# Later slots for the inverse-transform tables and a shifted forward burst in an FFT-mixing plus GELU-MLP kernel

## The chip, the cores and the metric

The kernel runs on one core of a Trainium2 chip. The metric is the device time of one execution in microseconds (us). The kernel before the change took 746.29 us, the median of three runs that lay between 744.68 and 748.18. A profiled execution took 745.42 us, 743.6 us of it from the first to the last instruction; its TensorE clock was granted in full over nearly the whole span.

In what follows PE is TensorE, ACT is ScalarE, DVE is VectorE, POOL is GpSimd and SP is SyncE, which here only issues DMAs.

## The reference, cut to what matters

```python
X = np.fft.rfft(x, axis=1)                       # x: (8, 3008, 256)
y = np.fft.irfft(X * (filt_r + 1j*filt_i), n=3008, axis=1)
h = y.reshape(24064, 256) @ w_in                 # w_in: (256, 2048)
out = (0.5*h*(1 + erf(h/sqrt(2)))) @ w_out       # w_out: (2048, 256)
```

Each of the eight batches is transformed along its 3008 positions, multiplied by a filter for each frequency and channel, and transformed back. The result goes, token by token, through a two-layer MLP with an exact GELU.

## The kernel before, in words

**The MLP.** The 24,064 tokens are cut into 47 tiles of 512. One tile is 16 steps of `mm1`: two matmuls of 512 columns into one PSUM bank (tag `h`, three banks), then a GELU on ACT that writes an f16 tile `g_sb` (L634, L637). The second layer of tile t runs while the first layer of tile t+1 does. For tile 0 it is the plain product, 64 matmuls of 256 columns (`mm2_first`, L647). From tile 1 on it is a seven-product scheme: 112 matmuls of 128 columns (`mm2_seven`, L706), fed by sums that DVE makes of `g_sb` (`sums_1` L675, `sums_2` L681, `sums_3` L688), with DVE combining the products into output tiles (L721 to L735). These use two PSUM banks with tag `o`, each in turn.

**The transforms.** 3008 = 47 x 64, so the transform of a batch is a chain of small matrix stages. Batch 0 is done ahead of the first tile. Each later batch is spread over the MLP tiles as bursts:

- `fold` (DVE, L106 and L107) makes sums and differences of the loaded input; `s1` (PE, L428) is the first stage. Its four PSUM banks, one of tag `h` and the three of tag `f`, are emptied two by DVE and two by ACT into `a_sb`, which SP writes to a DRAM scratch.
- `r1` reads it back in another order (`b_sb`, L444). `s2` (PE, L457) is the forward second stage. `s2_out` (DVE, L469) multiplies a bank of it by the filter `F` and writes a tile `p`. There are three such bursts for a batch, u = 0, 1, 2.
- `s3` (PE, L483) is the first inverse stage with the table `U`. `s3_out` empties its banks into `v_sb`, which goes to a second DRAM scratch (L496).
- `r2` reads that back (`d_sb`, L503). `s4` (PE, L512) is the last stage, with the table `T4a`; it writes 376 tokens of `y_sb`, from which `mm1` reads.

**The order.** It is written by hand. Time is cut into slots, 16 for a tile, and `put(slot, function, ...)` hangs a function on a slot. In each slot the functions hung there are issued first, then that slot's share of the second layer, then its `mm1`. One slot of the steady state issues 7 matmuls of the second layer and one `mm1`. Each engine works through its instructions in the order of issue, so an instruction that waits holds up all behind it on that engine. The bursts take the PSUM banks of tags `h` and `f` in turn, and wait until the earlier user's bank has been emptied.

**Tables made late.** `U` and the factors of `T4a` are needed only from batch 1 on. `table_4_factors` (L391: three small matmuls into one bank, three ACT copies) and `table_u` (L369: one matmul with `pick`, which POOL makes, and one ACT copy) run in tile 0, in slots 8 and 9, each in a bank of tag `o`. `mm2_first` begins at slot 9, also in the two `o` banks. `table_4_all` (POOL, L410 and L412) multiplies the factors out in four parts, from slot 10.

**Batch 1 and 2.** Tile 5 holds the last 448 tokens of batch 0 and the first 64 of batch 1. In slots 80 to 85 it has no `mm1`; the second layer of tile 4 takes 14 matmuls in each of these. Batch 1's third burst (`s2`, u = 2) is in slot 58, its `s3` in slot 67, and the `s4` of its first tokens in slots 80 to 83. Batch 2's folds are in slots 67, 69, 86 and 90, its `s1` in slots 89, 92, 96 and 100, and its first `s2` in slot 112.

Of the kernel before, what the change touches and what calls it, by code (L numbers as in the profile page):

```python
# [31 lines left out]
class _Mix:  # L32
# [332 lines left out]
        self.nc.gpsimd.tensor_scalar(out=self.pick, in0=to, scalar1=self.p, scalar2=None, op0=ALU.is_equal)  # L365

    def table_u(self):
        ps = self.bank("ps_u", "o")
        self.nc.tensor.matmul(ps[:, 0:128], lhsT=self.pick, rhs=self.u0.rearrange("p t r w -> p (t r w)"),  # L369
                              start=True, stop=True)  # L370
        self._evac(self.U.rearrange("p t r w -> p (t r w)"), ps[:, 0:128], "act")
# [15 lines left out]
                v.tensor_copy(out=self.T2g[:, r, :, j], in_=t[:, :, j, ::-1] if j else t[:, :, j])  # L387

    def table_4_factors(self, g):
        ps = self.bank("ps_t4", "o")  # L390
        mm = lambda o, n, t, k: self.nc.tensor.matmul(ps[0:96, o:o + n], lhsT=t, rhs=self.eye[0:k, 0:k], start=True, stop=True)  # L391
        for x in range(2):
            mm(NA * x, NA, self.T1g[:, x].rearrange("p r a j k -> p (r a j k)"), NA)
        mm(128, 128, self.T2g.rearrange("p r a j k -> p (r a j k)"), 128)
        t = self.t4
        self.G = t[:, 0:94].rearrange("p (x m) -> p x m", x=2)
        self.fcs = t[:, 96:224].rearrange("p (h w r) -> p w h r", h=2, r=2)
        self._evac(self.G[:, 0], ps[0:96, 0:NA], "act", self.wt[0:96])
        self._evac(self.G[:, 1], ps[0:96, NA:2 * NA], "act", self.wts[0:96])
        self._evac(t[:, 96:224], ps[0:96, 128:256], "act")  # L400
# [88 lines left out]
    def s3_out(self, b, u, i):  # L489
        ps = self.st[b, "ps3"][i]  # L490
        vt = self.pv.tile([128, 4, 256], BF16, tag="v", name="v_sb")
        for par in range(2):
            self._evac(vt[:, 2 * par:2 * par + 2, :].rearrange("p a b -> p (a b)"), ps[par],
                       "act")
        for q in range(2):
            self.nc.sync.dma_start(out=self.st[b, "R2"][:, 4 * u + 2 * i + q], in_=vt[64 * q:64 * q + 64])  # L496

# [277 lines left out]
def kernel(  # L775
# [9 lines left out]
    m = _Mix(ctx, tc, x, filt_r, filt_i, moe_w_in, moe_w_out, out)  # L785
# [4 lines left out]
    g = m.small  # L790
    wide = ctx.enter_context(ExitStack())
    m.psum(wide, w=(2, 1), m=(1, 1), n=(5, 1))
    act = "act"
# [109 lines left out]
    def put(slot, f, *a):  # L903
        at.setdefault(slot, []).append((f, a))

    def first(b):
        return (b * S // TCH) * 16

    busy, crowd, after = set(), set(), {}
    for b in range(1, B):  # L910
        hi = first(b)
        e = 4 * (b == B - 1)
        s1, n1, r1 = (4, 2.75, 16) if b == 1 else (hi - 87, 3.7, hi - 73) if b == 2 else (hi - 94 - e, 3.7, hi - 80 - e)
        s2 = (33, 45, 58) if b == 1 else (hi - 64 - 2 * e, hi - 48 - 3 * e + e // 4, hi - 32 - 3 * e)
        busy.update(range(s1 - 1, s1 + int(3 * n1) + 2))
        for c in range(4):
            slot = s1 + int(c * n1 + (b == 1 and c in (1, 2)))
            put((0, 1, 5, 8)[c] if b == 1 else (67, 69, 86, 90)[c] if b == 2 else s1 - 28 + e + 6 * c, m.fold, b, c)
            put(slot, m.s1, b, c)
            put(r1 if c < 3 else s2[0] + 1, m.r1, b, c)  # L920
        for u in range(3):
            put(s2[u], m.s2, b, u)
            for i in range(4):
                put(s2[u] + ((0, 2, 5, 6)[i] if b == u == 1 else 2 * i), m.s2_out, b, u, i // 2, i % 2)
            s3 = s2[u] + (9 if b == 1 and u != 1 else 10)
            put(s3, m.s3, b, u)
            put(s3 + 1, m.s3_out, b, u, 1)
            busy.update(range(s2[u] - 1, s2[u] + 5), range(s3 - 1, s3 + 2))
        after[b] = s3 + (5 if b > 1 else 4)
        crowd.update(range(s2[0], after[b]), range(s1 + 66, s1 + 94))  # L930
        if b + 1 < B:
            for i, (u, o, p) in enumerate(((0, 5, 2), (0, 7, 2), (1, 1, 4), (1, 5, 6), (1, 7, 6), (2, 1, 8), (2, 5, 10), (2, 7, 10))):
                put(s2[u] + o, m.load_next, b, p, i // 2, i % 2)

    for b in range(1, B):
        end = 1000000
        if b == B - 1:
            s4 = first(b) - 17
            for u in range(16):
                put(s4 + u, m.s4, b, u // 2, u % 2, act if u % 2 else False)  # L940
            for c in range(4):
                put(after[b] if c < 3 else s4 + 5, m.r2, b, c)
            continue
        for u in range(7, -1, -1):
            due = (b * S + GRP * u) // TCH * 16
            end = min(end, due - 2 if u or b > 1 else 81)
            if b == u == 1:
                end = 83
            for half in (1, 0):
                while end in busy:  # L950
                    end -= 1
                assert end > after[b] + 7
                put(end, m.s4, b, u, half, act if half or end in crowd or b == 1 and u == 0 else False)
                busy.add(end)
                end -= 1 if u < 3 else 2
            if u % 2 == 0:
                put(after[b] if u == 0 else end - 11, m.r2, b, u // 2)
# [2 lines left out]
    put(0, m.weights_4, g)  # L960
    put(0, m.table_u_pick, g)
    put(0, m.table_2_parities)
    put(8, m.table_4_factors, g)
    put(9, m.table_u)
    parts = [(w, h) for w in range(0, HB, 8) for h in range(2)]
    for i, slot in enumerate((10, 80, 96, 112)):
        put(slot, m.table_4_all, parts[2 * i:2 * i + 2])
    put(1, m.load_filters_again, nc.gpsimd, 0, 8)
    put(18, m.load_filters_again, nc.sync, 8, 16)
# [10 lines left out]
    for s in range((NT + 1) * 16):  # L980
        t, jc = s // 16, s % 16
        for f, a in at.pop(s, ()):
            f(*a)
        pace = lambda i: max(16 * (i - 6) // 10, 0) if t == late else i
        if t - 1 in seven:
            n = lambda i: (14 * i if i < 6 else 84 + 28 * (i - 6) // 10) if t == late else 7 * i
            m.mm2_seven(t - 1, n(jc), n(jc + 1))
        elif t < 2:
            n = lambda i: max(4 * i - 36, 0) if i < 16 else min(28 + 12 * (i - 16) // 5, 64)
            m.mm2_first(n(s), n(s + 1))  # L990
        for i in range(pace(jc), pace(jc + 1)) if t < NT else ():
            m.mm1(t, i)
# [31 lines left out]
```

## Time and profile before

| engine | busy us | share of the span |
|---|---|---|
| PE matmul | 722.8 | 97% |
| PE weight load | 507.2 | 68% |
| DVE | 583.1 | 78% |
| ACT | 575.5 | 77% |
| POOL | 292.9 | 39% |

The page gives for each engine the time in which it had an instruction at work, and the share of the span. Matmuls are pipelined, so a busy PE may still be waiting between starts. The timeline of one engine lists its instructions in order of time; a bracket at the end of a row gives the idle time ahead of it and what ended it. A table by stretches gives the busy time of every engine in each stretch of the span. Tile 0 begins at 38.5 us; the slots touched by the change lie between there and about 155 us.

A row of the timeline reads: start in us, duration in us, engine, line, operation, output and inputs, shape, how many; then, in brackets, the idle time before it and its releaser.

### The profile page before, as it was taken

The page shows a single profiled execution, that of the slowest core. Times are in us where ns is not written, and L with a number is a line of the kernel's source. Part 1 is how long each engine was busy: PE and PEld are TensorE (multiplying, and loading weights), DVE is VectorE, ACT ScalarE, POOL GpSimd, SP SyncE. Part 2 cuts the span into 40 slices and gives each one's busy share as a digit, 9 for nine tenths or more (in the row PEclk, how much of TensorE's full clock was granted, in tenths as well). Part 3 has the DMA queues.
Part 4 walks back from the last instruction along what each step waited for, and adds up shares of the span by engine and source line. Part 5 has one row for each costly group of instructions (what it writes and reads, how often), then busy time and mean ns, then how long its engine had stood idle before and what let it go on. Part 6 is the DMA issues. An engine that isn't in the chain of part 4 may idle for free.

```text
span 743.6 us, 20854 instructions
## 1 busy us (share of the span) xinstructions
PE 722.8 (97%) x8449; PEld 507.2 (68%) x8588; DVE 583.1 (78%) x1034; ACT 575.5 (77%) x1050; POOL 292.9 (39%) x546
## 2 busy tenths in 40 slices
PE   7989999999999999999999999999999999999997
PEld 4846666666776666666777666666677766777776
DVE  7876898888878797778976889778888887675666
ACT  6987777778887887778787777877788787777773
POOL 7994346675213453134611364115531112121121
PEclk9999999999999999999999999999999999999999
DMA  9999753746255652655536456255545443411011
GB/s 144 223 202 221 168 110 100 200 99 136 71 149 155 130 110 87 166 127 131 121 95 172 111 117 146 72 157 138 109 102 136 136 108 100 100 43 45 30 58 58
DMA packets 84051, 90.79 MB, mean 122 GB/s; under 512 B 13347, under 2 KB 63011, under 8 KB 83827
## 3 DMA queue, kind: packets, MB, share of 16 engines
q1 hardware_dynamic: 61011, 49.11, 25.7%
q0 software_dynamic: 22528, 40.15, 24.2%
q8 instruction: 67, 1.10, 0.6%
q14 instruction: 29, 0.24, 0.1%
q10 hardware_dynamic: 416, 0.20, 0.1%
HBM read 57.15 MB, written 48.23 MB: 142 GB/s over the span
## 4 chain that ended last, share of the span: by engine, by line
PE 82%; DMA 6%; ACT 5%; POOL 2%; DVE 2%; issue 2%; SPq 0%; DVEq 0%; POOLq 0%
PE ps_o L706 36%; PE ps_h L634 35%; PE ps_s L483 3%; PE ps_s L512 3%; ACT g_sb L637 3%; DMA x_sb<-in_x_dram 2%; PE ps_s L428 2%; PE ps_s L457 2%; ACT v_sb L329 1%; DMA d_sb<-R 1%; PE ps_o L647 1%; DMA F<-in_filt_i_dram 1%; POOL F L144 1%; ACT y_sb L329 1%; DMA R<-v_sb 1%
## 5 line engine op out<-in xcount | busy, mean ns | idle before, releaser
L637 ACT ACTIVATE g_sb<-ps_h 128x512 f16<-128x512 f32 x752 | 446.8, 602 | 148.4 <-PE ps_h L634 129.9
L634 PE MATMUL ps_h<-y_sb,w_in_sb 128*128 128x512 bf16 (+3 forms) x1465 | 417.1, 365 | 1.5 <-DVE a_sb L331 0.8
L753 POOL DMA_DIRECT2D out_dram<-ost x227 | 128.8, 574 | 387.1 <-DVE ost L735 366.2
L706 PEld LDWEIGHTS <-g_sb 128*128 128x128 f16 x2944 | 193.9, 98 | 82.0 <-issue 11.4
L706 PEld LDWEIGHTS <-s_sb 128*128 128x128 f16 x2208 | 148.0, 98 | 62.2 <-issue 11.1
L634 PEld LDWEIGHTS <-w_in_sb 128*128 128x128 bf16 x1600 | 125.1, 98 | 7.7 <-issue 2.1
L706 PE MATMUL ps_o<-w_sums,g_sb 128*128 128x128 f16 x1472 | 127.0, 219 | 0.9
L706 PE MATMUL ps_o<-w_sums,s_sb 128*128 128x128 f16 x1472 | 125.8, 219 | 1.6
L675 DVE TENSOR_TENSOR s_sb<-g_sb 128x1024 f16<-128x1024 f16 x184 | 120.9, 691 | 1.2 <-ACT g_sb L637 1.2
L706 PE MATMUL ps_o<-w_out_sb,g_sb 128*128 128x128 f16 x1472 | 119.2, 219 | 2.0 <-DVE ost L735 0.3
L469 DVE TENSOR_TENSOR p<-ps_s,F 128x1024 bf16<-128x1024 f32 x84 | 102.0, 1217 | 7.0 <-PE ps_s L457 5.4
L98 POOL DMA_DIRECT2D x_sb<-in_x_dram x156 | 79.0, 513 | 1.3 <-DMA x_sb<-in_x_dram 0.8
L728 DVE TENSOR_TENSOR t_sb<-t_sb,ps_o 128x256 f32<-128x256 f32 x46 | 19.3, 420 | 60.0 <-PE ps_o L706 60.0
L681 DVE TENSOR_TENSOR g_sb<-s_sb,g_sb 128x1024 f16<-128x1024 f16 x92 | 64.2, 699 | 1.6
L706 PE MATMUL ps_o<-w_out_sb,s_sb 128*128 128x128 f16 x736 | 63.8, 219 | 0.3
L688 DVE TENSOR_TENSOR s_sb<-g_sb 128x1024 f16<-128x1024 f16 x92 | 64.0, 696 | 0.0
L735 DVE TENSOR_TENSOR ost<-t_sb,ps_o 128x256 f32<-128x256 f32 x90 | 33.7, 415 | 21.1 <-PE ps_o L706 21.1
L512 PEld LDWEIGHTS <-d_sb 96*128 96x128 bf16 x448 | 31.8, 98 | 26.6 <-DMA d_sb<-R 0.9
L329 ACT ACTIVATE y_sb<-ps_s 128x376 bf16<-128x376 f32 x95 | 47.2, 497 | 1.6 <-PE ps_s L512 1.6
L329 ACT ACTIVATE v_sb<-ps_s 128x512 bf16<-128x512 f32 x84 | 45.5, 597 | 0.2
L331 DVE CAST a_sb<-ps_s 128x512 bf16<-128x512 f32 x54 | 34.7, 684 | 12.4 <-PE ps_s L428 12.0
L512 PE MATMUL ps_s<-T4a,d_sb 96*128 96x94 bf16 x448 | 38.0, 206 | 1.9 <-DMA d_sb<-R 0.6
(154 smaller groups left out, 503.7 us busy)
## 6 DMA issues: line engine op xcount, KB each, us to landing
out_dram<-ost POOLq DMA_DIRECT2D x125, 128.0 KB, 2.3
b_sb<-R SPq DMA_DIRECT2D x28, 384.0 KB, 3.9
R<-v_sb SPq DMA_DIRECT2D x84, 128.0 KB, 2.4
d_sb<-R SPq DMA_DIRECT2D x56, 192.0 KB, 3.6
R<-a_sb SPq DMA_DIRECT2D x108, 96.0 KB, 2.2
x_sb<-in_x_dram POOLq DMA_DIRECT2D x48, 94.0 KB, 2.7
x_sb<-in_x_dram POOLq DMA_DIRECT2D x48, 48.0 KB, 2.7
x_sb<-in_x_dram POOLq DMA_DIRECT2D x12, 188.0 KB, 5.4
```

Source lines behind the costliest of these rows:

```text
L98: self.nc.gpsimd.dma_start(out=xt[64 * v + to:64 * v + to + m, h, 4 * c:4 * c + 4 * n, :], in_=xv[h][at:at + m, w:w + 4 * n, :])
L329: self.nc.scalar.activation(out=out, in_=in_, func=AF.Copy, scale=1.0 if scale is None else scale)
L331: self.nc.vector.tensor_copy(out=out, in_=in_)
L469: self.nc.vector.tensor_tensor(out=self.st[b, "w"][:, :, d:4:2, :], in0=ps.unsqueeze(1).to_broadcast([128, 2, 2, 256]), in1=self.F[:, :, k ...
L512: nc.tensor.matmul(ps[:, 94 * i:94 * i + 94], lhsT=d[:, (grp % 2) * 4 + i, 128 * half:128 * half + 128], rhs=self.T4a[:, 4 * grp + i], sta ...
L634: nc.tensor.matmul(ps[:, o:o + n], lhsT=w[:, dc], rhs=self.ring[:, dc, off:off + n], start=(dc == 0), stop=(dc == 1))
L637: nc.scalar.activation(out=self.st["g", t][:, jc, :], in_=ps, func=AF.Gelu)
L675: self.nc.vector.tensor_tensor(out=self.st["s", t][:, i:i + 2], in0=a, in1=b, op=ALU.subtract)
L681: self.nc.vector.tensor_tensor(out=a21[:, k], in0=self.st["s", t][:, k, 0], in1=a22[:, k], op=ALU.add)
L688: self.nc.vector.tensor_tensor(out=self.st["s4", t][:, k], in0=a12[:, k], in1=s2[:, k], op=ALU.subtract)
L706: nc.tensor.matmul(ps[:, (m + 1) % 2, sub, :], lhsT=a[:, i, 128 * sub:128 * sub + 128], rhs=b[:, i], start=i == 0, stop=i == 7)
L753: eng.dma_start(out=out, in_=tile_[lo - r0:lo - r0 + n])
```

## The change

It moves work between slots and between two kinds of PSUM banks; the arithmetic is the same.

1. `table_4_factors` goes from slot 8 to 14, `table_u` from 9 to 18, the first part of `table_4_all` from 10 to 15. Both tables take a bank of tag `f` instead of `o`.
2. `mm2_first` begins at slot 10 instead of 9, and has 24 instead of 28 matmuls issued by slot 16. It still ends with slot 31.
3. Batch 1: the third burst moves from slot 58 to 57 and its `s2_out`, `s3`, `s3_out` and `r2` with it. One of the four emptyings of the second burst's `s3` moves from ACT to DVE. The `s4` of the first tokens moves from slots 80 to 83 to slots 82 to 85.
4. Batch 2: the fourth fold moves from slot 90 to 94. The first `s2` moves from 112 to 113, its `s2_out` by two slots, to 114, and its `s3` by one. Some `s4` and `r2` of batch 1 around it follow, by one to three slots.

The purpose is to take the tables out of the stretch where tile 0 starts, and to give the DRAM round trips of batches 1 and 2 another distance to the bursts that use them.

```diff
 def table_u(self):
-    ps = self.bank("ps_u", "o")
+    ps = self.bank("ps_u", "f")
...
 def table_4_factors(self, g):
-    ps = self.bank("ps_t4", "o")
+    ps = self.bank("ps_t4", "f")
...
 def s3_out(self, b, u, i):
...
-                   "act")
+                   False if b == u == i == par == 1 else "act")
...
-    s2 = (33, 45, 58) if b == 1 else (hi - 64 - 2 * e, hi - 48 - 3 * e + e // 4, hi - 32 - 3 * e)
+    s2 = (33, 45, 57) if b == 1 else (hi - 64 - 2 * e + (b == 2), hi - 48 - 3 * e + e // 4, hi - 32 - 3 * e)
...
-        put((0, 1, 5, 8)[c] if b == 1 else (67, 69, 86, 90)[c] if b == 2 else s1 - 28 + e + 6 * c, m.fold, b, c)
+        put((0, 1, 5, 8)[c] if b == 1 else (67, 69, 86, 94)[c] if b == 2 else s1 - 28 + e + 6 * c, m.fold, b, c)
...
-            put(s2[u] + ((0, 2, 5, 6)[i] if b == u == 1 else 2 * i), m.s2_out, b, u, i // 2, i % 2)
+            put(s2[u] + ((0, 2, 5, 6)[i] if b == u == 1 else 2 * i + (b == 2 and u == 0)), m.s2_out, b, u, i // 2, i % 2)
...
-        end = min(end, due - 2 if u or b > 1 else 81)
+        end = min(end, due - 2 if u or b > 1 else 83)
         if b == u == 1:
-            end = 83
+            end = 85
...
-put(8, m.table_4_factors, g)
-put(9, m.table_u)
+put(14, m.table_4_factors, g)
+put(18, m.table_u)
...
-for i, slot in enumerate((10, 80, 96, 112)):
+for i, slot in enumerate((15, 80, 96, 112)):
...
-        n = lambda i: max(4 * i - 36, 0) if i < 16 else min(28 + 12 * (i - 16) // 5, 64)
+        n = lambda i: max(4 * i - 40, 0) if i < 16 else min(24 + 8 * (i - 16) // 3, 64)
         m.mm2_first(n(s), n(s + 1))
```

## The prediction

> **What bounds the kernel now.** I read the page's engine shares first, then the table by stretches, then the PE timeline around each slot that the diff names, and last the DVE timeline where PE waited for DVE.
>
> ```profile
> PE 722.8 (97%) x8449; PEld 507.2 (68%) x8588; DVE 583.1 (78%) x1034; ACT 575.5 (77%) x1050; POOL 292.9 (39%) x546
> ```
>
> ```profile
> 38.00:46.00 8.00, 6.58 (x47) 2.63 (x48) 7.86 (x14) 7.94 (x20) 7.39 (x23) 1.00 1.15 190
> ...
> 205.00:700.00 495.00, 488.80 (x5800) 346.04 (x5896) 386.02 (x681) 389.04 (x710) 157.72 (x301) 1.00 0.46 116
> ```
>
> After the stretch itself, the columns are PE, weight loads, DVE, ACT, POOL, the granted clock, the DMA share and GB/s. From 205 to 700 us PE is busy 488.8 of 495 us, and the diff leaves the order there alone: nothing is to be had. From 38 to 46 us it is busy only 6.58 of 8. So the change is worth what it takes from or adds to the PE waits between 38 and 155 us. These are the ones near its slots (PE timeline; the bracket is idle time and releaser):
>
> ```profile
> 42.62 0.59 PE L634 MATMUL ps_h<-y_sb,w_in_sb 128*128 128x512 bf16 x2 [0.53 <-DVE a_sb L331]
> ...
> 45.84 0.23 PE L369 MATMUL ps_u<-u,pick 128*128 128x128 bf16 x1 [0.72 <-POOL pick L365]
> ...
> 46.53 0.27 PE L647 MATMUL ps_o<-w_out_sb,g_sb 128*128 128x256 f16 x1 [0.35 <-ACT U L329]
> ```
>
> ```profile
> 97.63 0.45 PE L706 MATMUL ps_o<-w_out_sb,g_sb 128*128 128x128 f16 x5 [0.33 <-DVE ost L735]
> ```
>
> ```profile
> 110.77 0.34 PE L512 MATMUL ps_s<-T4a,d_sb 96*128 96x94 bf16 x4 [0.46 <-DMA d_sb<-R]
> ```
>
> ```profile
> 142.12 0.30 PE L457 MATMUL ps_s<-b_sb,T2p 64*64 64x256 bf16 x4 [0.29 <-DMA b_sb<-R]
> ```
>
> The brackets count from the modelled end of the matmul before. By starts, which I use below, a wait is about 0.17 longer: 0.89 and 0.51 us for the two table waits, 0.49 for the output tile, 0.63 at 110.77, 0.45 at 142.12. The five that the diff aims at sum to 2.97 us, 0.40% of 746: the ceiling of the gain.
>
> **What the Trainium skill says.** "Perfetto Trace Analysis", section Identifying the Most-Contended Engine, says that busy time of matmuls is no good measure of headroom because they are pipelined; the trace agrees (the 0.49 us wait shows as 0.33), so I count from start to start. "SBUF — State Buffer", section SBUF: two separate sides, says that a DVE operation with two SBUF inputs and a POOL operation lock each other out of one port pair for a whole instruction. The trace agrees: L681 takes 0.68 us at 128.17 and 1.20 at 130.12, beside POOL's table products. So a delayed DVE chain keeps its slow members.
>
> **Part 1, tables and first second-layer matmuls.** Removed from the path: the wait for `pick` (0.89) and that for the copy of `U` (0.51), 1.40 us. At slot 18 `pick`, ready at 45.8, is long there, and an `f` bank is free; at slot 14 likewise. PE still does the four small matmuls (about 0.3 us) and ACT the four copies (some 0.9 us), now beside slots where PE takes 0.7 to 0.86 us and ACT one GELU of 0.6: hidden. But the waits also gave DVE time. With them gone PE reaches `mm1` 9 at 44.67 instead of 46.86. That `mm1` takes the `h` bank of the second `s1`, which DVE empties from 44.41 to 45.05: a new wait of 0.4. The third `s1` starts at about 45.6 and finds its second DVE bank just emptied (45.69): 0.1. The fourth `s1` starts at about 48.1 and needs a bank of the third. DVE can empty that only after the fold that ends at 47.19 plus two casts of 0.65, at 48.5: 0.2 in its second half. So 0.7 comes back and **0.7 us is gained** (0.3 if DVE is later, 1.3 if those waits don't appear). The wait at 42.62 hangs on folds that stay: unchanged.
>
> **Part 2, batch 1's third burst.** The wait at 97.63 is PE needing an `o` bank that L735 frees. DVE before:
>
> ```profile
> 90.40 1.23 DVE L469 TENSOR_TENSOR p<-ps_s,F 128x1024 bf16<-128x1024 f32 x1 [1.80 <-PE ps_s L457]
> ...
> 95.10 1.22 DVE L469 TENSOR_TENSOR p<-ps_s,F 128x1024 bf16<-128x1024 f32 x1
> 96.23 0.68 DVE L675 TENSOR_TENSOR s_sb<-g_sb 128x1024 f16<-128x1024 f16 x1
> 96.83 0.74 DVE L735 TENSOR_TENSOR ost<-t_sb,ps_o 128x256 f32<-128x256 f32 x2
> 97.49 1.21 DVE L469 TENSOR_TENSOR p<-ps_s,F 128x1024 bf16<-128x1024 f32 x1
> ```
>
> Read from it: 7.17 us from the first filter product to the end of L735, with three of the four products ahead of it. Afterwards all four are ahead, since the fourth goes from slot 64 to 63: 7.17 + 1.17 = 8.34. The start comes one slot (0.82) earlier, at 89.58, so L735 ends at 97.92, later than 97.57. PE no longer asks at 97.14, though: `s3`, now in slot 66, is issued ahead of that slot's second layer and takes 1.1 us, so the question comes at about 98.3. **The wait of 0.49 goes.** The extra cast on DVE (0.65) fits in the 1.80 us of idle. Its bank is wanted one slot later by `s2`; an ACT bank of the same burst comes free at about 89.4, where `s2` wants it at 89.3: 0.1 lost. Net 0.4.
>
> **Part 3, first tokens of batch 1.** `s3` ends about 1.3 us earlier, `s4` comes two slots of 0.78 later: the round trip has nearly 3 us more and the wait of 0.63 goes. The second layer of tile 4, however, then runs ahead without pause, and soon needs the sums L681 makes:
>
> ```profile
> 110.97 0.69 DVE L675 TENSOR_TENSOR s_sb<-g_sb 128x1024 f16<-128x1024 f16 x1 [0.31 <-ACT g_sb L637]
> 111.58 1.28 DVE L681 TENSOR_TENSOR g_sb<-s_sb,g_sb 128x1024 f16<-128x1024 f16 x2
> ```
>
> Their start hangs on the last GELU of tile 4, which stays. Matmul 36 of the tile needs the second L681, done at 112.86. PE would start the tile at 110.14 and reach it 36 x 0.0555 us and one `s4` (0.2) later, at 112.34: a wait of about 0.53 takes the place of the 0.63. **Net 0.1.**
>
> **Part 4, batch 2.** A fold is L106 + L107, 1.4 us. DVE behind its old place has only 0.52 us of idle before 131.24; the 0.9 left over delays the chain down to the casts of the fourth `s1`, from 131.57 to about 132.45. Behind those casts SP queues the last scratch writes, and behind these the reads of `b_sb`. So `b_sb` lands 0.9 later, `s2` asks 0.82 later, and the wait of 0.45 stays or moves: on the way the second L681 of tile 5 would end at 132.2, where PE wants it at 131.87. `s2_out`, a slot later, frees its `h` bank at about 144.8 for an `mm1` due at 144.74. **Net 0.15 lost** (from 0.45 gained to 0.9 lost).
>
> **Sum.** 0.7 + 0.4 + 0.1 − 0.15 = 1.05 us, 0.14%: 746.29 − 1.05 = **745.2 us**.
>
> **The rivals.** (a) The waits go and nothing takes their place, 2.97 less the 0.1: 743.4 us. For it: all five releasers are moved or outrun. Against: DVE is busy 7.86 of 8 us in the first stretch. (b) DVE becomes the bound: the displaced fold costs 0.9, the early second burst finds its banks full (0.5), part 1 is eaten by casts (gain 0.3), L735 still waits, part 3 brings nothing. Sum 1.1 slower: 747.4 us. For it: the tight DVE chains above. Against: each displaced piece has some slack downstream. (c) Nothing is seen: the PE waits only change place, 746.3.
>
> **How the numbers follow.** Forecast 0.5, (a) 0.2, (b) 0.15, (c) 0.15. Runs of the kernel before scatter by up to 1.9 us about their median, so each case is widened by about that. The range 742.4 to 748.2 holds (a) and (b) with most of their scatter. Faster by over 0.5% means below 742.56, beyond the whole ceiling of 2.97 us, so it needs scatter or something I did not see: 0.19. Slower by over 0.5% means above 750.0: (b) and its scatter, 0.08. Within: 0.73.
>
> **What would show it.** After: no wait of PE for `pick`, for `U` or for `d_sb` in tile 5; in tile 0 waits of 0.1 to 0.4 us for casts by DVE ahead of `mm1` 9 and the fourth `s1`; no wait for L735 at slot 66; a new wait of PE for L681 near 112 us; a wait for `b_sb` or L681 near 132 to 142 still there; everything from 205 us on about 1 us earlier. I am wrong if PE from 38 to 155 us gains more than 2 us or loses any, or if the steady part changes its length.

## The result, and the profile after

The changed kernel takes 744.08 us (median of 17 runs, 743.46 to 745.13). The kernel before took 746.49 in the same comparison (17 runs, 744.68 to 749.85). The ratio is 0.9964, with a 95% interval of 0.9954 to 0.9975: 2.4 us less, where 1.05 was forecast. A second comparison, the last row but one of the table below, gave 744.13 (19 runs) against 745.43 (48 runs), ratio 0.9977 [0.9967, 0.9986]. The scatter has shrunk too: a standard deviation of 0.39 us against 1.37 in the first comparison.

The profiled run after took 743.85 us, 742.1 of it from the first to the last instruction. The engine shares and the same two stretches:

```profile
PE 722.6 (97%) x8448; PEld 507.7 (68%) x8588; DVE 585.2 (79%) x1036; ACT 574.9 (77%) x1048; POOL 293.3 (40%) x546
```

```profile
38.00:46.00 8.00, 6.74 (x50) 2.40 (x47) 7.86 (x13) 7.66 (x17) 7.39 (x23) 1.00 1.13 188
205.00:700.00 495.00, 488.91 (x5802) 346.12 (x5898) 385.48 (x678) 389.13 (x708) 157.98 (x300) 1.00 0.46 115
```

The steady part is what it was (488.91 us of PE against 488.80). In the first stretch PE gained 0.16 us. The list of what PE waited for shows what stayed (line and releaser, then total us, times and longest):

```profile
PE ps_o L706 <- DVE g_sb L681: 0.9, 2, 0.7
PE ps_h L634 <- DVE a_sb L331: 0.7, 2, 0.6
...
PE ps_h L634 <- ACT g_sb L637: 0.6, 1, 0.6
```

`pick`, `U`, L735, `d_sb` in tile 5 and `b_sb` are gone from it. Three waits are new. One is in tile 0, where PE now reaches `mm1` 9 before a GELU has emptied its bank (timeline of PE):

```profile
42.33 0.59 PE L634 MATMUL ps_h<-y_sb,w_in_sb 128*128 128x512 bf16 x2 [0.58 <-DVE a_sb L331]
...
45.08 0.59 PE L634 MATMUL ps_h<-y_sb,w_in_sb 128*128 128x512 bf16 x2 [0.62 <-ACT g_sb L637]
```

One is near 111 us and is shown with part 3 below. The longest is in batch 2's stretch (timeline of all engines):

```profile
128.60 2.57 DVE L681 TENSOR_TENSOR g_sb<-s_sb,g_sb 128x1024 f16<-128x1024 f16 x1
...
128.99 1.62 POOL L410 TENSOR_TENSOR tmp_sb<-t_sb 96x376 f32<-96x376 f32 x2
...
131.22 0.51 PE L706 MATMUL ps_o<-w_sums,g_sb 128*128 128x128 f16 x6 [0.73 <-DVE g_sb L681]
```

To place the gain I compared the start of each of the 752 GELUs (L637) in the profile of before with the same GELU in two profiles of the changed kernel, and took the difference over each stretch. The first column of measurements is the profile above, the second that of the later run of the same kernel.

| stretch | forecast gain, us | measured | measured again |
|---|---|---|---|
| tile 0, and tile 1 until it settles (part 1) | 0.7 | 0.75 | 0.73 |
| batch 1's third burst (part 2) | 0.4 | 0.30 | 0.31 |
| first tokens of batch 1 (part 3) | 0.1 | 0.11 | 0.12 |
| batch 2 up to 134 us (part 4) | −0.15 for all of part 4 | −0.90 | −0.89 |
| from there to tile 8 (`b_sb` wait of before, absent) | in the line above | 0.49 | 0.35 |
| near 226 us (a `d_sb` wait of before, absent) | none | 0.32 | 0.33 |
| sum from the start of tile 0 | 1.05 | 1.07 | 0.95 |

From 240 us to the end the difference doesn't change. So these pairs of profiles hold about the 1.05 us of the forecast, but only because the two waits of before in the lines near 140 and 226 us, which the forecast did not count as gained, nearly make up for the loss in part 4. The start of tile 0 lay 0.4 and 0.5 us earlier in these runs; other kernels that leave everything ahead of it alone lay between 0.6 earlier and 1.3 later, so I count that as scatter. The experiments had to answer two questions: where the further 1.3 us between the medians are, and whether parts 1 to 4 did what their terms say.

### The profile page after: what moved, and what is told of

Same layout as the page of the kernel before. It is cut to its first block, busy times and chain, and to the rows that moved or that the text cites. A ratio compares the mean times of both kernels' runs of the same rounds, so it can differ in the third digit from the quotient of the medians.

```text
span 742.1 us, 20855 instructions
## 1 busy us (share of the span) xinstructions
PE 722.6 (97%) x8448; PEld 507.7 (68%) x8588; DVE 585.2 (79%) x1036; ACT 574.9 (77%) x1048; POOL 293.3 (40%) x546
## 4 chain that ended last, share of the span: by engine, by line
PE 85%; ACT 6%; DVE 3%; DMA 2%; issue 2%; POOL 1%; DVEq 0%; POOLq 0%
PE ps_o L706 38%; PE ps_h L634 37%; PE ps_s L483 3%; ACT g_sb L637 3%; PE ps_s L512 3%; DMA x_sb<-in_x_dram 2%; PE ps_s L428 2%; PE ps_s L457 2%; ACT v_sb L329 1%; PE ps_o L647 1%; POOL F L144 1%; DVE g_sb L681 1%; ACT y_sb L329 1%; DVE s_sb L675 1%; ACT b_sb L329 0%
## 5 line engine op out<-in xcount | busy, mean ns | idle before, releaser
L637 ACT ACTIVATE g_sb<-ps_h 128x512 f16<-128x512 f32 x752 | 446.7, 601 | 146.3 <-PE ps_h L634 127.7
L675 DVE TENSOR_TENSOR s_sb<-g_sb 128x1024 f16<-128x1024 f16 x184 | 121.1, 692 | 1.0 <-ACT g_sb L637 1.0
L681 DVE TENSOR_TENSOR g_sb<-s_sb,g_sb 128x1024 f16<-128x1024 f16 x92 | 65.1, 708 | 1.6
L735 DVE TENSOR_TENSOR ost<-t_sb,ps_o 128x256 f32<-128x256 f32 x90 | 33.8, 417 | 20.6 <-PE ps_o L706 20.5
L723 DVE TENSOR_TENSOR ost<-t_sb,ps_o 128x256 f32<-128x256 f32 x46 | 19.1, 416 | 26.1 <-PE ps_o L706 26.1
```

What stands on the lines that cost most here:

```text
L637: nc.scalar.activation(out=self.st["g", t][:, jc, :], in_=ps, func=AF.Gelu)
L675: self.nc.vector.tensor_tensor(out=self.st["s", t][:, i:i + 2], in0=a, in1=b, op=ALU.subtract)
L681: self.nc.vector.tensor_tensor(out=a21[:, k], in0=self.st["s", t][:, k, 0], in1=a22[:, k], op=ALU.add)
```

## The experiments

Each was compared with runs of the kernel before on the same chip; three chips served, and medians from different chips are compared with more caution. The column "dropped runs" counts the runs whose mean granted TensorE clock was under 0.999; its reason, and its limits, come with part 4 alone. Parts are numbered as in the prediction. The recorded expectations number them as the list under "The change" does: their parts 1 and 2 are part 1 here, and their part 3 is parts 2 and 3 here.

| kernel | median us (runs) | before, same chip | ratio [95%] | dropped runs |
|---|---|---|---|---|
| part 1 alone | 744.39 (18) | 746.36 | 0.9973 [0.9960, 0.9986] | 3 of 18 |
| parts 2 and 3 alone | 745.04 (22) | 746.36 | 0.9986 [0.9973, 0.9999] | 8 of 22 |
| part 4 alone | 746.70 (14) | 746.36 | 1.0003 [0.9987, 1.002] | 5 of 14 |
| parts 1 to 3 | 743.37 (11) | 746.36 | 0.9952 [0.9936, 0.9968] | 0 of 11 |
| `pick` first | 747.48 (22) | 746.31 | 1.0015 [1.0003, 1.0027] | 18 of 22 |
| `pick` late | 753.64 (4) | 746.31 | 1.0097 [1.0069, 1.0125] | 4 of 4 |
| changed kernel, fold back at 90 | 743.32 (13) | 746.31 | 0.9961 [0.9949, 0.9973] | 0 of 13 |
| part 1 and the burst, `s4` not moved | 743.73 (16) | 746.31 | 0.9962 [0.9951, 0.9973] | 0 of 16 |
| before, four matmuls more in slot 9 | 746.05 (14) | 745.43 | 0.9995 [0.9981, 1.0008] | 1 of 14 |
| tables moved, second layer at slot 9 | 744.01 (15) | 745.43 | 0.9980 [0.9967, 0.9992] | 1 of 15 |
| changed kernel again | 744.13 (19) | 745.43 | 0.9977 [0.9967, 0.9986] | 1 of 19 |
| fold back at 90 again | 743.45 (13) | 745.43 | 0.9967 [0.9956, 0.9978] | 0 of 13 |

**Part 1 alone.**

```diff
-    ps = self.bank("ps_u", "o")
+    ps = self.bank("ps_u", "f")
...
-    ps = self.bank("ps_t4", "o")
+    ps = self.bank("ps_t4", "f")
...
-put(8, m.table_4_factors, g)
-put(9, m.table_u)
+put(14, m.table_4_factors, g)
+put(18, m.table_u)
...
-        n = lambda i: max(4 * i - 36, 0) if i < 16 else min(28 + 12 * (i - 16) // 5, 64)
+        n = lambda i: max(4 * i - 40, 0) if i < 16 else min(24 + 8 * (i - 16) // 3, 64)
```

> Parts 1 and 2 of the change alone: the two tables in f banks at slots 14 and 18, the second layer of tile 0 from slot 10; batches 1 and 2 as before. The trace pair gives 0.74 us for this stretch. Theory of the PE waits: 0.7 us faster than before, about 745.7 against 746.5, and the scatter of the runs stays that of before (some 5 us from lowest to highest, against 1.7 of the changed kernel), since the DRAM round trips are as before. Rival (all of the gain sits in tile 0, and the scatter with it): 2 to 2.5 us faster and a scatter below 2 us.

Measured: 2.0 us less in the median, near the rival's number; the runs spread over 2.3 us. In its profile tile 0 gains 0.74 us, as in the changed kernel. So the median holds more than the profile's tile 0. The wait for `b_sb` was absent here too, though nothing of batch 2 is touched.

**Parts 2 and 3 alone, part 4 alone, parts 1 to 3.** The edits are those lines of the diff: the `s2` slot 57 with one `s3_out` on DVE and the `s4` at 82 to 85; then the fold at 94 with `s2` at 113; then all but the latter.

> Part 3 alone: batch 1's third burst a slot earlier with one cast on DVE, and the s4 of its first tokens two slots later; tables and batch 2 as before. Theory of the PE waits by the two traces: 0.4 + 0.1 = 0.5 us faster, scatter unchanged. Theory of the landing time: the wait of PE for d_sb in tile 5 varies from run to run with the DRAM round trip, the profile caught a short one, and taking it off the path brings 1.0 to 1.8 us and narrows the scatter from some 5 us to 2 or 3.

> Part 4 alone: the fourth fold of batch 2 at slot 94, its first s2 at 113, the products at 114; tables and batch 1 as before. The trace pair shows a new wait of 0.9 us for L681 and the wait of 0.45 for b_sb gone. Theory of the PE waits: 0.3 to 0.5 us slower than before, scatter unchanged. Theory that the rest of the gain hangs on the landing of b_sb: 0.5 to 1 us faster, scatter narrower.

> The changed kernel without part 4: fold of batch 2 at 90, first s2 at 112, products from 112. Theory of the PE waits: the 0.9 us wait for L681 goes and 0.45 for b_sb comes back, so 0.4 us faster than the changed kernel, 743.7. Theory that part 4 matters for the landing of b_sb: slower than the changed kernel by 0.3 to 0.8 and with a wider scatter.

Measured: 1.3 us less, 0.3 more (not told from nothing) and 3.0 less. Parts 2 and 3 alone brought the size that the rival theory named, but their runs still spread over 5.1 us, which it denied. Parts 1 to 3 without part 4 are 0.7 us better than the whole change, if medians from two chips may be compared. The profile of part 4 alone then gave the first answer. It has a longer wait for `pick` than the profile of before (timeline of PE):

```profile
46.60 0.24 PE L369 MATMUL ps_u<-u,pick 128*128 128x128 bf16 x1 [1.72 <-POOL pick L365]
...
47.79 1.06 PE L634 MATMUL ps_h<-y_sb,w_in_sb 128*128 128x512 bf16 x2
```

The same two `mm1` matmuls took 0.59 us elsewhere, and 1.06 here. The granted clock, the third number from the end in these one-microsecond stretches of the same run, says why:

```profile
46.00:47.00 1.00, 0.40 (x2) 0.19 (x3) 0.79 (x2) 0.20 (x2) 1.00 (x2) 0.84 1.03 268
47.00:48.00 1.00, 0.85 (x5) 0.55 (x4) 0.00 (x0) 0.15 (x1) 0.94 (x3) 0.50 1.05 285
48.00:49.00 1.00, 1.00 (x6) 0.19 (x8) 0.00 (x0) 0.11 (x1) 0.94 (x3) 0.50 0.59 159
49.00:50.00 1.00, 1.00 (x10) 0.16 (x3) 0.48 (x1) 0.93 (x2) 0.94 (x3) 0.50 0.03 4
50.00:51.00 1.00, 1.00 (x8) 0.70 (x7) 0.81 (x2) 0.64 (x3) 1.00 (x3) 0.95 0.02 3
```

After an idle stretch of 1.89 us (start to start) the clock was halved for about 3.4 us: 0.16 + 3 x 0.5 + 0.05 = 1.71 us of clock lost, twice that at half speed. This kernel's tile 0 lost 2.3 us against the profile of before: 1.0 of longer wait and the rest at half clock. Nothing in its edit lies ahead of 100 us. Of the longer wait, 0.76 is `pick` coming later, because POOL was slower in that run (timelines of POOL, before and part 4 alone); the rest is PE asking earlier:

```profile
44.62 0.19 POOL L262 TENSOR_TENSOR wts<-wt,h 128x1 f32<-128x1 f32 x1
44.76 0.30 POOL L362 IOTA cols<- 128x128 f32 x1
45.16 0.63 POOL L365 TENSOR_SCALAR pick<-cols,p 128x128 bf16<-128x128 f32 x1
```

```profile
44.88 0.19 POOL L262 TENSOR_TENSOR wts<-wt,h 128x1 f32<-128x1 f32 x1
45.02 0.30 POOL L362 IOTA cols<- 128x128 f32 x1
45.42 1.12 POOL L365 TENSOR_SCALAR pick<-cols,p 128x128 bf16<-128x128 f32 x1
```

The same instruction took 0.63 and 1.12 us. Half a clock for 3.4 us is 0.0023 of the mean over 744 us, so such a run shows a mean clock of 0.998 or less, and I count a run under 0.999 as dropped. **Of 144 runs of before in three comparisons, 52 lie under it; their median is 747.74 us, that of the other 92 is 745.38. Of 36 runs of the changed kernel one does.** The limit does not separate cleanly, because the mean also holds the end of the span, where half clock costs nothing as PE has finished. In the fourteen profiles PE ends about 4.2 us before the span does and the clock fell no sooner than 2.0 us after that, so the end takes at most some 1.1 us of clock, 0.0015 of the mean (an estimate from these profiles): 0.998 can mean either, 0.997 or less means half clock earlier on. At 0.997 or less lie 40 of the 144 and 1 of the 36, so the contrast stands. The profile of before (745.42 us) happened to catch a run with no drop.

The Trainium skill has this gate: "TensorE: Matmul & The Clock Gate", section What's actually happening, gives half clock after an idle window of about 3.4 us, and a window that runs free of the program. The 3.4 us at 0.50 agree, and a free-running window fits that only some runs drop. But here 1.89 us of idle were enough, so the full idle window that the page asks for isn't needed.

**`pick` first, `pick` late.** If the wait for `pick` is all there is to it, POOL making it first should do as well as moving the tables; making it last should cost more.

```diff
+    put(0, m.table_u_pick, g)
     put(0, m.table_4_rows, g)
     put(0, m.weights_4, g)
-    put(0, m.table_u_pick, g)
```

This is the first. In the second, the same line stands behind POOL's other tables of slot 0.

> The kernel before, with one line moved: POOL makes pick ahead of the other table rows of slot 0, so that it is ready some 7 us before table_u asks for it. Slots, banks and second layer as before. Theory of the idle PE (the wait for pick varies from 0.6 to 1.9 us from run to run, and a long one is followed by some 3.4 us of TensorE at half clock): most of what the tables part brought, 1.3 to 2.0 us faster than before, no run with a mean clock below 0.999, scatter below 2.5 us; the wait of 0.5 for the copy of U stays. Theory that the o bank and the early second layer matter more: at most 0.7 us faster, scatter as before.

> The kernel before, with pick made after the eight copies of T2p on POOL (4.8 us later). PE then waits some 5.5 us for it in tile 0. Theory of the idle PE: every run shows half clock after the wait, so the time is the added wait (about 4.8) and 1 to 1.7 us more than the runs of before without a clock drop: 750.5 to 752 us, and the profile has a stretch of 3.4 us at 0.5. Theory without the clock: 4.8 us above the median of before, 751.2, clock 1.0 throughout, scatter as before.

My theory of the first fell. Its profile:

```profile
46.27 0.27 PE L647 MATMUL ps_o<-w_out_sb,g_sb 128*128 128x256 f16 x1 [1.70 <-ACT t_sb L329]
```

`pick` was early, but the other table's `o` bank is emptied by an ACT copy that needs `wts` from the same POOL chain, and the first second-layer matmul needs that bank. The wait was not shorter (1.87 us by starts), only renamed, and 18 of 22 runs dropped, 13 of them to 0.997 or less. The profiled run is one of the 18, but its clock fell only at the end of the span, 2.0 us after its last matmul, and was whole behind the wait (stretches):

```profile
46.00:50.00 4.00, 3.35 (x26) 1.72 (x25) 2.00 (x3) 2.99 (x8) 3.83 (x8) 1.00 0.50 133
...
740.00:742.00 2.00, 0.14 (x3) 0.00 (x0) 0.46 (x2) 0.00 (x0) 0.00 (x0) 1.00 0.68 197
742.00:744.00 2.00, 0.00 (x0) 0.00 (x0) 0.00 (x0) 0.00 (x0) 0.00 (x0) 0.53 0.02 4
```

So a wait near 1.9 us brings the drop in some runs and not in others. With `pick` late, PE waited much longer (timeline, then one stretch):

```profile
51.08 0.29 PE L369 MATMUL ps_u<-u,pick 128*128 128x128 bf16 x1 [6.34 <-POOL pick L365]
```

```profile
47.00:57.00 10.00, 5.77 (x26) 2.62 (x27) 1.40 (x3) 2.56 (x5) 8.94 (x18) 0.50 0.57 144
```

All four runs dropped, and the time rose by 7.3 us. The clock halved inside the wait, at 47.0 us, and came back at 57.2, three times 3.4 us later; PE worked for 6.2 us of it. That is why 753.64 lies above the 750.5 to 752 expected, where one stretch of 3.4 us was priced. So a longer idle stretch does bring the drop. Making `pick` early is not enough; whether the change needs the later slot, the other kind of bank or both, no run separates.

**Four matmuls more.** The clock can be tested apart from the wait: keep the wait, and fill part of it with work.

```diff
+    def keep_warm(self, n):
+        ps = self.bank("ps_warm", "f")
+        for i in range(n):
+            self.nc.tensor.matmul(ps, lhsT=self.ones[:, 0:128], rhs=self.ones, start=True, stop=True)
...
+put(9, m.keep_warm, 4)
 put(9, m.table_u)
```

> The kernel before, with four matmuls of 512 columns more (their result is not used) in slot 9 of tile 0, ahead of the matmul that waits for pick. Nothing waits less: the added 0.9 us of PE work lies inside the wait for pick. Theory (the wait for pick is what lets the granted clock fall in part of the runs of before): with the idle stretch shortened to under 1 us, at most 1 run in 10 has a mean clock below 0.999 (of before about 4 in 10 have), and the median is 745.2 to 745.8, the time of those runs of before whose clock did not fall, about 0.8 us below before. Rival (the clock is not the cause; the 1.3 us beyond the forecast come from the order of work): median as before or up to 0.5 us slower, with as many runs below 0.999 as before.

The clock went the way of the theory: one run of 14 dropped, against 14 of 48 of before, and the standard deviation fell from 1.29 to 0.57 us. The counts alone are thin: with no effect, so few would come up about once in twelve times. In the profile `pick` came nearly as late as in part 4's run (46.34 against 46.60), PE had idled 1.02 us from start to start instead of 1.89, and the clock stayed whole (timeline, then one stretch):

```profile
46.34 0.23 PE L369 MATMUL ps_u<-u,pick 128*128 128x128 bf16 x1 [0.86 <-POOL pick L365]
```

```profile
46.00:50.00 4.00, 3.35 (x26) 1.79 (x27) 1.86 (x3) 2.38 (x5) 3.82 (x9) 1.00 0.69 183
```

The median was a miss: 746.05, above the 745.2 to 745.8 expected. In the profile this kernel lost 0.96 us in tile 0 against before, all of it the later `pick` and what followed. Over runs without a drop it is about as much slower: 746.01 us against 745.12. So what the clock gave back, the edit took elsewhere. The drop was priced, but not that a slow POOL still makes the wait itself longer, nor that four matmuls (0.86 us) outlast a short wait; how these two share the miss is not shown. Taken together, the long wait with every run dropped, the filled wait with one in 14 and the moved tables with few or none show the idle stretch as the cause of the drop. It costs in its own right as well.

**Tables moved, second layer at slot 9.** Part 1 without its later start of the second layer: `n(i)` is left as before.

> Part 1 without the later start of the second layer: the tables go to slots 14 and 18 and to f banks, but mm2_first begins at slot 9 as in before. If it is the tables alone that matter: 744.4, as the kernel with parts 1 and 2 of the diff's tile 0 (2.0 us below before), no clock below 0.999. If the later start is needed (PE would reach the GELUs of tile 0 one slot earlier and wait for them): 744.7 to 745.5, with a PE wait for g_sb (ACT L637) near 42 to 45 us that is longer by 0.3 or more.

744.01 us; the ratio's interval overlaps with that of part 1. Tile 0 gained 0.96 us in its profile. The later start isn't needed for the gain.

**Fold back at 90; `s4` not moved.** The first is the changed kernel with one number undone; the second is part 1 with the third burst alone.

```diff
-            put(... (67, 69, 86, 94)[c] if b == 2 ...
+            put(... (67, 69, 86, 90)[c] if b == 2 ...
```

> The changed kernel with batch 2's fourth fold back at slot 90 (its s2 stays at 113). If the displaced fold makes the 0.9 us wait for L681, that wait goes and the b_sb wait stays away: 0.7 us faster than the changed kernel, 743.4, like the kernel without part 4. If the later s2 and its products cost, no gain: 744.1.

> The kernel without part 4 and with the s4 of batch 1's first tokens back in slots 80 to 83. Trace theory: s4 finds d_sb (the burst is a slot earlier), the wait for L681 at slot 82 is smaller, so within 0.3 us of the kernel without part 4 (743.4). Theory of the landing time: d_sb is again late in some runs, 0.3 to 0.8 us slower than that kernel.

> The changed kernel once more, on one chip with the next one. 744.1, 2.3 us below before; PE waits 0.7 us at 131 for L681.

> The changed kernel with the fourth fold of batch 2 back in slot 90. Theory: the fold in slot 94 pushes the second L681 of tile 5 back, so this kernel is 0.6 to 0.9 us faster than the changed one of the same call (743.3 against 744.1). Rival: the two earlier medians differed by chance; they are equal within 0.3 us here.

With the fold at 90 the kernel took 743.32 and, beside the changed kernel on one chip, 743.45 against 744.13: 0.7 us better, as expected. Near 131 us its PE has no wait, where the changed kernel loses 0.9. The DVE timeline there:

```profile
127.03 0.68 DVE L681 TENSOR_TENSOR g_sb<-s_sb,g_sb 128x1024 f16<-128x1024 f16 x1
127.63 1.31 DVE L675 TENSOR_TENSOR s_sb<-g_sb 128x1024 f16<-128x1024 f16 x1
128.98 1.20 DVE L681 TENSOR_TENSOR g_sb<-s_sb,g_sb 128x1024 f16<-128x1024 f16 x1
```

and that of the changed kernel:

```profile
127.28 0.68 DVE L681 TENSOR_TENSOR g_sb<-s_sb,g_sb 128x1024 f16<-128x1024 f16 x1
127.88 0.69 DVE L675 TENSOR_TENSOR s_sb<-g_sb 128x1024 f16<-128x1024 f16 x1
128.60 2.57 DVE L681 TENSOR_TENSOR g_sb<-s_sb,g_sb 128x1024 f16<-128x1024 f16 x1
```

PE stood 1.14 us ahead of before in the first and 1.53 in the second. Counted in before's time, L675 starts at 128.77 and 129.41: the displaced fold has set this chain back by 0.64. L675 makes it up, with 0.69 us instead of 1.31, so the second L681 starts at 130.12 and 130.13. But it takes 2.57 us instead of 1.20, and ends 1.38 later. With the fold at 90, POOL's product L410 began at 128.34 (129.48 in before's time) and met first L675, then L681; with it at 94 L410 began at 128.99 (130.52), a microsecond later, and L681 alone ran beside it. Both profiles of the changed kernel and that of part 4 alone show 2.56 to 2.57. Why POOL's product came later stands in the POOL timelines, of before and of the changed kernel:

```profile
126.62 2.83 POOL L753 DMA_DIRECT2D out_dram<-ost  x5 [5.82 <-DVE ost L735]
129.47 2.54 POOL L410 TENSOR_TENSOR tmp_sb<-t_sb 96x376 f32<-96x376 f32 x2
```

```profile
126.13 2.85 POOL L753 DMA_DIRECT2D out_dram<-ost  x5 [6.86 <-DVE ost L735]
128.99 1.62 POOL L410 TENSOR_TENSOR tmp_sb<-t_sb 96x376 f32<-96x376 f32 x2
```

It follows the same five issues of output transfers, and these wait for an L735 that DVE, behind the displaced fold, ends 1.05 us later. That the meeting with L410 is what stretches L681 is read from the durations; no run moves POOL's product alone.

Without the move of `s4` the kernel took 743.73 against 743.37 with it, 0.36 us; the two come from different chips, and a difference of this size between chips tells neither theory from the other. **The fold at 90 with all the rest beats both kernels: 743.45 us, against 744.13 and 745.43 on the same chip, ratio to before 0.9967 [0.9956, 0.9978].**

## Why the prediction was right, and where it wasn't

The medians fell by more than the forecast, inside the range. The means of all runs recorded with their clocks differ by 2.16 us (746.31 and 744.15). By the numbers above, 745.38 − 744.10 = 1.28 us separate runs without a drop, and 1.00 on the one chip that ran both (745.12 and 744.12), close to the forecast's 1.05; and 0.36 x (747.74 − 745.38) = 0.85 is what the dropped runs of before cost (0.70 if only those at 0.997 or less are counted). **The term that was missing is this 0.7 to 0.85**: the working read one profile, and took the wait for `pick` (0.89) for what it always is. The scatter of before, 744.68 to 748.18 in the three runs on record, was widened into the range and not asked for a cause. And that the rest comes so near to 1.05 is in part luck, as parts 3 and 4 show.

- *Part 1, 0.7.* Size right (0.73 to 0.75), inner terms not. By starts, from 41 to 56 us, PE's waits sum to 2.29 us before and 1.54 after. Removed: `pick` 0.89, `U` 0.51, and one of 0.20 near 54.7 us that the working left alone. New: 0.79 ahead of `mm1` 9, forecast 0.4 and for a DVE cast; it was for a GELU, since ACT too had been given time by the old wait. The 0.1 ahead of the third `s1` did not come, and neither did the 0.2 in the fourth. A gap of 0.22 stands in the profile after near 48 us, but there a record is missing: PE has 8448 matmuls in it for 8588 weight loads, and each missing `mm1` leaves such a gap. Part 1 alone, with all 8588 recorded, has none there.
- *Part 2, 0.4.* The wait for L735 went; 0.30 to 0.31.
- *Part 3, 0.1.* The wait for `d_sb` went, and two for the sums of L681 took its place, by starts 0.21 for the first and 0.37 for the second; one of 0.53 was forecast. Net 0.11. The PE timeline after has the second as:

```profile
111.50 0.51 PE L706 MATMUL ps_o<-w_sums,g_sb 128*128 128x128 f16 x6 [0.21 <-DVE g_sb L681]
```

- *Part 4, −0.15.* The step that failed is "the second L681 of tile 5 would end at 132.2, where PE wants it at 131.87", a wait of 0.33. It was 0.90, since that L681 ended at 132.70 in before's time; PE asked when forecast. The displaced fold did set the chain back, by 0.64 at L675, but L675 then lost its slow duration and L681 more than doubled its own. The working cited the lock of "SBUF — State Buffer" (section SBUF: two separate sides), but kept before's durations, "slow members" and all, instead of asking which member would meet POOL after the shift. A second error made up for it: the 0.45 wait for `b_sb`, which "stays or moves", was absent. It was absent too in most profiles of kernels whose batch 2 is untouched, but `pick` first has it with 0.43. Like the `d_sb` wait near 226 us, it varies from run to run or depends on the timing of the work ahead of it; which of the two stays open.
- *Rivals.* The median lies nearer to the number of (a), 743.4, than to the forecast, but its mechanism fell: tile 0 has a new wait of 0.79 and batch 2 one of 0.90. (b) fell: DVE is at 79%, and parts 1 to 3 gained. (c) fell with the interval of the ratio.
- *Parts against medians.* Parts 1 to 3 were forecast at 1.2 us. Over runs without a drop they gave 745.40 − 743.37 = 2.0, where the profile shows 1.15 in the changed places and 0.82 in the `b_sb` wait and the one near 226 us. Parts 2 and 3 alone agree in the same way: 1.0 over runs without a drop, 1.0 from tile 0 on in the profile; part 1 alone has 1.0 and 1.2. That suggests that the waits for `b_sb` and near 226 us were typical of before and not a chance of its one profile. Part 4 then took 0.7 back. The net came out nearly right because an underrated gain and an underrated loss cancelled, which is luck.

## What to carry to other kernels

When a kernel scatters more than its neighbours, look at each run's granted clock before costing a wait from one profile, and at where in the span the clock was lost: a wait of PE that is close to 2 us in some runs may cost nearly twice its length. Moving one producer earlier does not remove a wait while another table shares the banks and the producing engine; find the second releaser first. And when a DVE operation is put elsewhere, ask not only what is delayed, but which operation will then run beside POOL.

## What the runs showed of the hardware

- 1.89 us without a matmul were followed by about 3.4 us at half clock in one profile, and 1.87 us by none in another (`pick` first, where 13 of 22 runs still fell to 0.997 or less). With 1.02 us idle in the profile, one run in 14 dropped. At the end of the span the clock fell 2.0 us after the last matmul in one profile (`pick` first).
- With 6.34 us idle the half clock lasted 10.2 us, three times 3.4, and went on for 6.2 us after PE had work again.
- A small POOL operation took 0.63 or 1.12 us (L365) in different runs of the same instructions.
- L681 took 0.68 us alone, 1.20 across the end of the first and the start of the second of POOL's two products, 2.57 when it began 0.39 us ahead of the first. The two products took 2.54 us together beside L675 and L681, and 1.62 beside the long L681. That the earlier start did not keep L681 short differs from what "SBUF — State Buffer" states in section SBUF: two separate sides, that whichever starts first holds the ports; the measured durations decide here.
